# One inversion for four tiles' sums, a bound from sums for w_out on ScalarE, and another order, in attention with two MoE layers

## The chip, the cores and the metric

The kernel runs on one core of one Trainium2 chip. The metric is device time of one execution in microseconds, the median over runs.

## The reference

Queries are averaged in pairs of neighbouring positions, so 1152 positions give 576 queries for each of 4 batches and 8 heads. Attention runs over 1152 keys with head size 64. Its result, 2304 tokens by 512, goes through two layers without a residual.

```
q_pool = q.reshape(B, H, S // 2, 2, D).mean(axis=3)
scores = q_pool @ k.T / sqrt(D);  attn = exp(scores - max(scores))
x = (attn / (sum(attn) + 1e-9)) @ v            # (2304, 512)
h = x @ w_in;   x = (h * sigmoid(h)) @ w_out   # MoE1, 512 -> 2048 -> 512
x = (((x @ w1) * (x @ w2)) @ w3) @ w_out2      # MoE2, 512 -> 1024 -> 1024 -> 512
```

Weights arrive as 64-bit floats. Queries and keys are drawn larger by 5.8 than the rest of the attention's inputs.

## The kernel before

**Numbers.** Most products run on pairs of 16-bit floats, a high and a low part, in three terms: high x high, high x low, low x high. To split a tensor the kernel needs a power of two near its largest magnitude. So a maximum along each partition is taken, TensorE spreads it over the partitions (`top_mm`, L387 and L390), and a scale follows. A weight chunk of 128 x 512 first becomes f32 (`from_f64`): GpSimd L406, ScalarE L412, and two merge instructions on VectorE, L416 and L417. It is then split by ScalarE (L926) and VectorE (L931) and written back by a DMA, 16 chunks for w_in and 16 for w_out (`weights_moe1`). Each chunk's maximum is L903, on VectorE.

**Attention.** A tile is 128 queries of one head, or the 64 last ones of two heads: 144 tiles, 36 for each batch, in groups of four and a fifth in every second group. `tile_ops` gives a tile's steps: scores (TensorE L585, f32, into one of two PSUM tiles `sc` of three banks), the negated maximum over 1152 keys (VectorE L631), the exponential with its running sum (ScalarE L606), one over that sum (VectorE L611 and L614). In the first batch (`whole`) the exponentials stay f32. TensorE transposes them, nine blocks of 128 x 128, into one of the same two `sc` tiles (L643); ScalarE copies the result out (L646); the attention output is a product of 36 f32 matmuls (L677); and the inverses are applied afterwards: four small matmuls spread them over the partitions (L684), ScalarE copies (L697), VectorE multiplies (L702). In the other three batches the inverse scales the split of the exponentials (L652, L617), a DMA transposes them, and the output is L736.

**MoE layers.** A block is 256 tokens, nine blocks in all. `block_ops` makes eight hidden units for each (24 matmuls, L819), the gate by a tanh (ScalarE L835, VectorE L838), the split of the gated values (ScalarE L841, GpSimd L844), and 16 output units (12 matmuls, L860). A hidden unit reads four w_in chunks, an output unit four w_out chunks. MoE2 comes last, in six blocks of 384 tokens: products with w1 and w2 (L1326), w3 times w_out2 computed once (L1183), and the final product (L1404). w1 and w2 are split in two halves of chunks after a spread maximum each; there an Abs with a running sum on ScalarE (L1096) already stands for the maximum.

**What sets the order.** No loop is executed as written. `Plan.op` records every operation with its engine, a cost, a key (its due time, in tiles) and the buffers it reads and writes. `timed` plays the plan through with those costs: on every engine that operation goes next which can start and has the lowest key. `run` does this once with the written keys, and then once for each number of `DRAWS`. A number seeds a random change of the keys: a pull towards the latest time that the last plan allows, an offset for a few kinds of operation, or noise in one stretch. Each pass starts from the keys of the one before it. The order of the last pass is what each engine gets, one queue in program order per engine, DMAs on SyncE's. So a different list gives another order from the first instruction to the last.

```
keys = [o.key for o in self.ops]
order = self.timed(keys)
for n in DRAWS:
    keys = self.draw(n, keys, order)
    order = self.timed(keys)
```

## Time and profile before

| | |
|---|---|
| runs | 1115.26, 1116.67, 1119.01 us (median 1116.67) |
| profiled execution | 1118.18 us; its span, first to last instruction, 1116.4 us |
| TensorE busy | 1071.2 us, 96% |
| VectorE busy | 792.0 us, 71% |
| ScalarE busy | 692.4 us, 62% |
| GpSimd busy | 160.3 us, 14% |
| mean granted clock of TensorE | 0.994 of full speed |

The profile's page shows shares over the whole span. A matmul on the page is one instruction; the weight loads that go with it are PEld and run beside it. The view by stretch cuts the span into windows. The grouped view adds up instructions of one line, operation and shape. The timeline lists an engine's instructions in order of time and joins neighbours of one kind, with their count behind the x. The chain of waits is followed back from the last instruction.

### The profile page before, as it was taken

The numbers are of one execution on the slowest core, as the hardware profiler recorded it, in microseconds if no ns is written. First come the engines' busy times: TensorE is split into PE (matmuls) and PEld (weight loads), VectorE is DVE, ScalarE is ACT, GpSimd is POOL, SyncE is SP. The second block draws the span as 40 slices with busy tenths as digits, with TensorE's granted clock in tenths as the row PEclk, the third lists the DMA queues.
The fourth block names the chain that finished last, engine by engine and source line by source line (L and its number), as shares of the span: only waits on it lengthen the run. The fifth ranks groups of instructions, "written<-read, shape, count | busy, mean of one in ns | idle before, by whom it ended". The sixth has DMA issues, their size and how long they took to land.

```text
span 1116.4 us, 22719 instructions
## 1 busy us (share of the span) xinstructions
PE 1071.2 (96%) x9356; PEld 816.9 (73%) x9356; DVE 792.0 (71%) x1304; ACT 692.4 (62%) x1103; POOL 160.3 (14%) x150
## 2 busy tenths in 40 slices
PE   4877999999999999999999999999999999999998
PEld 4655778888888888788788888788777655555553
DVE  5999997798787897887889784789956442332311
ACT  4767768677776786686687775676656433242322
POOL 1310220021020020020021120546210000000000
PEclk8999999999999999999999999999999999999999
DMA  9855517499998999999989987664530010100001
GB/s 355 263 168 196 190 51 243 91 197 196 199 199 168 188 208 203 207 186 206 202 159 190 168 147 126 218 189 143 189 113 29 29 48 20 38 20 19 19 10 57
DMA packets 294823, 163.21 MB, mean 146 GB/s; under 512 B 256064, under 2 KB 266816, under 8 KB 294720
## 3 DMA queue, kind: packets, MB, share of 16 engines
q1 hardware_dynamic: 294720, 161.77, 60.6%
q8 instruction: 73, 1.20, 0.4%
q14 instruction: 30, 0.25, 0.1%
HBM read 80.22 MB, written 9.44 MB: 80 GB/s over the span
## 4 chain that ended last, share of the span: by engine, by line
PE 53%; DMA 4%; DVE 1%; POOL 1%; issue 0%; ACT 0%; ACTq 0%; POOLq 0%; SPq 0%
PE mt L1326 13%; PE mt L1404 6%; PE mm L819 6%; PE mm L860 6%; PE sc L585 4%; PE mm L1326 4%; PE mm L736 4%; DMA pt<-p 3%; PE mt L1183 3%; PE mt L860 3%; PE mm L1404 2%; PE mt L819 1%; PE mm L1183 1%; DMA v<-in_moe_w_dram 1%; POOL g L844 1%
## 5 line engine op out<-in xcount | busy, mean ns | idle before, releaser
L631 DVE TENSOR_REDUCE sm<-sc 128x1 f32<-128x1152 f32 x144 | 192.2, 1350 | 35.7 <-PE sc L585 35.3
L606 ACT ACTIVATE e<-sc,sm 128x1152 f32<-128x1152 f32 x144 | 175.0, 1216 | 52.7 <-DVE sm L631 43.8
L585 PE MATMUL sc<-kt,qt 64*128 64x384 f32 (+3 forms) x1280 | 183.1, 427 | 17.8 <-ACT pt L646 11.0
L860 PEld LDWEIGHTS <-w 128*128 128x128 f16 x1728 | 166.3, 98 | 31.2 <-issue 11.4
L819 PEld LDWEIGHTS <-w 128*128 128x128 f16 x1728 | 166.4, 98 | 28.2 <-issue 8.6
L844 POOL TENSOR_TENSOR g<-t,g 128x512 f16<-128x512 f32 x72 | 100.4, 1402 | 527.9 <-ACT g L841 475.7
L585 PEld LDWEIGHTS sc<-kt,qt 64*128 64x128 f32 (+1 forms) x1280 | 139.2, 178 | 49.3 <-issue 14.5
L617 DVE SCALAR_TENSOR_TENSOR p<-e,sm,p 128x1152 f16<-128x1152 f32 x108 | 161.2, 1500 | 12.8 <-ACT p L652 12.4
L860 PE MATMUL mm<-g,w 128*128 128x256 f16 x1440 | 167.1, 273 | 0.0
L819 PE MATMUL mm<-x,w 128*128 128x256 f16 x1440 | 165.0, 273 | 1.9 <-DVE x L783 1.0
L652 ACT ACTIVATE p<-e,sm 128x1152 f16<-128x1152 f32 x108 | 134.1, 1251 | 40.6 <-DMA pt<-p 26.0
L736 PE MATMUL mm<-pt,v 128*64 128x256 f16 (+1 forms) x1944 | 89.1, 248 | 3.6 <-DMA pt<-p 3.4
L736 PEld LDWEIGHTS <-v 128*64 128x64 f16 x1944 | 80.7, 111 | 12.3 <-issue 10.8
L1326 PEld LDWEIGHTS <-w1h 128*128 128x128 f16 x576 | 56.1, 98 | 38.3 <-issue 0.8
L1326 PEld LDWEIGHTS <-w2h 128*128 128x128 f16 x576 | 56.0, 98 | 38.2 <-issue 1.4
L1326 PE MATMUL mt<-x2h,w1h 128*128 128x384 f16 x444 | 77.1, 326 | 0.0
L1326 PE MATMUL mt<-x2h,w2h 128*128 128x384 f16 x444 | 76.9, 326 | 0.0
L643 PE MATMUL sc<-identr,e 128*128 128x128 f32 x324 | 44.6, 286 | 14.4 <-ACT e L606 11.3
L835 ACT ACTIVATE t<-mm,xm 128x512 f32<-128x512 f32 x60 | 40.9, 682 | 22.8 <-PE mm L819 20.1
L1345 ACT ACTIVATE asb<-mt,x2m 128x384 f32<-128x384 f32 x37 | 20.8, 577 | 54.4 <-PE mt L1326 48.0
L643 PEld LDWEIGHTS sc<-identr,e 128*128 128x128 f32 x324 | 36.7, 146 | 22.7 <-ACT e L606 14.6
L646 ACT COPY pt<-sc 128x1152 f32<-128x1152 f32 x36 | 40.0, 1116 | 18.8 <-PE sc L643 18.4
(186 smaller groups left out, 1331.4 us busy)
## 6 DMA issues: line engine op xcount, KB each, us to landing
v<-in_moe_w_dram SPq DMA_DIRECT2D x32, 512.0 KB, 4.3
qs<-in_q_dram SPq DMA_DIRECT2D x16, 640.0 KB, 4.8
kt<-in_k_dram SPq DMA_DIRECT2D x16, 576.0 KB, 4.6
qs<-in_q_dram SPq DMA_DIRECT2D x16, 512.0 KB, 4.8
g<-in_moe_w_in_dram SPq DMA_DIRECT2D x16, 512.0 KB, 5.5
w<-t SPq DMA_DIRECT2D x32, 256.0 KB, 2.4
stage<-in_v_dram SPq DMA_DIRECT2D x12, 576.0 KB, 5.1
x2d<-t SPq DMA_DIRECT2D x36, 128.0 KB, 2.4
```

The lines of the kernel that those rows point to most:

```text
L585: return nc.tensor.matmul(sc.t[cols, bank, x0 - bank * (S // 3) : x1 - bank * (S // 3)], qt.t[rows * D : (rows + 1) * D, 4 if last else 2 ...
L606: nc.scalar.activation(e.t.rearrange("p (a x) -> p a x", a=3), flat(), AF.Exp, bias=sm.t[:, 0:1], accum_out=sm.t[:, 1:2])
L617: nc.vector.scalar_tensor_tensor(p16.t[:, 1], e.t, sm.t[:, 3:4], p16.t[:, 0], op0=ALU.mult, op1=ALU.subtract)
L631: DVE, 1.36, lambda: nc.vector.tensor_reduce(sm.t[:, 0:1], flat(), axis=AX.XY, op=ALU.max, negate=True),
L643: nc.tensor.transpose(to[:, c * P : (c + 1) * P], e.t[:, c * P : (c + 1) * P], ident)
L652: ACT, 1.27, lambda: nc.scalar.activation(p16.t[:, 0], e.t, AF.Copy, scale=sm.t[:, 3:4]),
L736: nc.tensor.matmul(ps.t[a * D : (a + 1) * D, :nn], v16.t[:, a, c, tv, :], rhs, start=idx == 0, stop=idx == 3 * NK - 1,)
L819: nc.tensor.matmul(ps.t[:, f % 2 * BL : (f % 2 + 1) * BL], w16[0][ct * NQ + f // 4][:, tw, (f % 4) * P : (f % 4 + 1) * P], x16.t[:, ct, tx ...
L844: nc.gpsimd.tensor_tensor(gv(1), two(g32), gv(0), op=ALU.subtract)
L860: nc.tensor.matmul(ps.t[:, :BL], w16[1][f][:, tw, ct * P : (ct + 1) * P], gs[u].t[:, f % 4, tg, :], start=f == 0 and n == 0, stop=f == NF ...
L1326: nc.tensor.matmul(ps.t[:, :TB], buf.t[:, ct, tw, f * P : (f + 1) * P], xr.t[:, ct, tx, :], start=idx == 0, stop=idx == 11,)
L1404: nc.tensor.matmul(ps.t, ab[f].t[:, ta, m * P : (m + 1) * P], w3_b.t[:, f, tb, :], start=f == 0 and n == 0, stop=f == NF2 - 1 and n == 2,)
```

## The change

Three things change.

The four whole tiles of a group in the first batch write their sums into four columns of one small tile `gs`, and after the fourth, one add and one reciprocal of 128 x 4 stand for four pairs of 128 x 1. The spread reads its columns. The fifth tile of a group, and all tiles of later batches, keep their own pair.

For w_out, the chunk's maximum on VectorE becomes an Abs on ScalarE that sums the row as it goes. The scale is then a power of two from the largest sum over 512 magnitudes, which is at least the largest magnitude. w_in keeps its maximum.

The list of draws is another and longer one, 87 numbers where there were 33.

```diff
--- before.py
+++ after.py
@@ -30,9 +30,15 @@
 LOAD_AFTER = 3.0
 SLACK = 3.0
 DRAWS = (
-    200001, 200004, 200006, 200007, 200012, 200017, 200034, 200040, 200060, 200094, 200118, 200122,
...
+    3000001, 3000002, 3000004, 3000006, 3000008, 3000014, 3000020, 3000032, 3000041, 3000050,
...
 )
 SWITCH = 0.1
 AFTER = {PE: 0.25, ACT: 0.2, DVE: 0.15, POOL: 0.2, SP: 0.0}
@@ -334,7 +340,8 @@
     t_pt = tags(attn, "pt", 3, [P, 2, 2 * NK, P], F16)
     t_x32 = tags(attn, "x32", 1, [P, NP, BL])
     t_x32t = tags(attn, "x32t", 1, [P, NP, BL])
-    t_sm = tags(attn, "sm", 12, [P, 4])
+    t_sm = tags(attn, "sm", 8, [P, 4])
+    t_gs = tags(attn, "gs", 2, [P, 3, 4])
     t_mv = tags(attn, "mv", 2, [P, 6, NP])
     t_rs = tags(attn, "rs", 1, [P, BL])
 
@@ -558,7 +565,7 @@
 
     pts = {}
     x32s = {}
-    dgs = {}
+    dgs, sums = {}, {}
     turns, asked = {}, {}
 
     def pt32(pt):
@@ -602,10 +609,21 @@
                 tc.add_to_no_dep_group(f"bank{paired[0]}", first.ins)
                 tc.declare_fence(second.ins, group=f"bank{paired[0]}")
 
+        joint = whole and not last
+        if joint and (b, g, hp) not in sums:
+            sums[(b, g, hp)] = attn_buf(t_gs)
+        n = 2 * h + j - 2 * g
+
         def soft_exp():
+            to = sums[(b, g, hp)].t[:, 0, n : n + 1] if joint else sm.t[:, 1:2]
             nc.scalar.activation(
-                e.t.rearrange("p (a x) -> p a x", a=3), flat(), AF.Exp, bias=sm.t[:, 0:1], accum_out=sm.t[:, 1:2]
-            )
+                e.t.rearrange("p (a x) -> p a x", a=3), flat(), AF.Exp, bias=sm.t[:, 0:1], accum_out=to
+            )
+
+        def inverses():
+            s_ = sums[(b, g, hp)].t
+            nc.vector.tensor_scalar(s_[:, 1], s_[:, 0], 1e-9, None, op0=ALU.add)
+            nc.vector.reciprocal(s_[:, 2], s_[:, 1])
 
         def inverse():
             nc.vector.tensor_scalar(
@@ -631,11 +649,15 @@
             DVE, 1.36, lambda: nc.vector.tensor_reduce(sm.t[:, 0:1], flat(), axis=AX.XY, op=ALU.max, negate=True),
             [sc], [(sm, 0)], i - 0.5,
         )
-        op(ACT, 1.42, soft_exp, [sc, (sm, 0)], [e, (sm, 1)], i - 3.0 * whole)
-        op(DVE, 0.32, inverse, [(sm, 1)], [(sm, 2)], i + 0.2)
+        op(ACT, 1.42, soft_exp, [sc, (sm, 0)], [e, (sums[(b, g, hp)], n) if joint else (sm, 1)], i - 3.0 * whole)
+        if not joint:
+            op(DVE, 0.32, inverse, [(sm, 1)], [(sm, 2)], i + 0.2)
+        elif n == 3:
+            s_ = sums[(b, g, hp)]
+            op(DVE, 0.32, inverses, [(s_, c) for c in range(4)], [(s_, 9)], i + 0.2)
         if whole:
             st = Buf(t_s)
-            dgs[i] = sm
+            dgs[i] = (sums[(b, g, hp)], n) if joint else (sm, None)
 
             def turn32():
                 to = st.t.rearrange("p a x -> p (a x)")
@@ -679,11 +701,11 @@
                     )
 
         def spread():
-            for (a, jj), dg in inv.items():
+            for (a, jj), (dg, n) in inv.items():
                 cols = slice(a * TAIL, (a + 1) * TAIL) if last else slice(0, P)
                 nc.tensor.matmul(
                     sp.t[a * D : (a + 1) * D, jj * P : jj * P + (TAIL if last else P)],
-                    dg.t[:, 3:4].to_broadcast([P, D]),
+                    (dg.t[:, 3:4] if n is None else dg.t[:, 2, n : n + 1]).to_broadcast([P, D]),
                     ident[:, cols],
                     start=True,
                     stop=True,
@@ -691,7 +713,7 @@
 
         sp, rs = Buf(t_mm), attn_buf(t_rs)
         first = op(
-            PE, 0.3 if last else 0.6, spread, [ident_b] + [(dg, 2) for k_, dg in inv.items() if not last or k_ == (0, 0)],
+            PE, 0.3 if last else 0.6, spread, [ident_b] + [(dg, 2 if n is None else 9) for k_, (dg, n) in inv.items() if k_ == (0, 0)],
             [sp, (rs, 0)], i + 1.0,
         )
         op(ACT, 0.3 if last else 0.45, lambda: nc.scalar.copy(rs.t[:, :nn], sp.t[:, :nn]), [sp], [(rs, 1)], i - SOON)
@@ -898,13 +920,23 @@
 
             op(SP, 0.5, load, [], [(w64, 0), (w64, 1)], key - 3, land=5.5).ready = 45.0 * wi
             from_f64(lambda c=c: whole[c], words, w16_b[wi][c], w64, key)
-            op(
-                DVE, 0.69,
-                lambda c=c: nc.vector.reduce_max(
-                    wmx[wi][:, c : c + 1], whole[c], axis=AX.X, apply_absolute_value=True
-                ),
-                [w16_b[wi][c]], [(wmx_b[wi], c)], key + 0.02,
-            )
+            if wi == 0:
+                op(
+                    DVE, 0.69,
+                    lambda c=c: nc.vector.reduce_max(
+                        wmx[wi][:, c : c + 1], whole[c], axis=AX.X, apply_absolute_value=True
+                    ),
+                    [w16_b[wi][c]], [(wmx_b[wi], c)], key + 0.02,
+                )
+            else:
+                junk = moe_buf(t_t32)
+                op(
+                    ACT, 0.66,
+                    lambda c=c, junk=junk: nc.scalar.activation(
+                        junk.t, whole[c], AF.Abs, accum_out=wmx[wi][:, c : c + 1]
+                    ),
+                    [w16_b[wi][c]], [junk, (wmx_b[wi], c)], key + 0.02,
+                )
             key += step
         s_ = wst[wi]
         op(DVE, 0.2, lambda: nc.vector.reduce_max(s_[:, 0:1], wmx[wi], axis=AX.X), [wmx_b[wi]], [wst_b[wi]], key2)
```

What stands where in the engines' queues changes from the beginning. In the rows below `sc` are the two score tiles, `sm` a tile's small column of maximum, sum and inverse, `e` exponentials, `w_0_n` chunk n of w_in, `g` the 64-bit words of a chunk, `wmx` the column of chunk maxima. First VectorE, around the maxima of the third and fourth tile, before:

```order
L631 TENSOR_REDUCE sm_120<-sc_82 128x1
L416 SCALAR_TENSOR_TENSOR w_0_3_145<-w_0_3_145,g_177 128x512
L417 SCALAR_TENSOR_TENSOR w_0_3_145<-g_177,w_0_3_145 128x512
L416 SCALAR_TENSOR_TENSOR w_0_2_144<-w_0_2_144,g_176 128x512
L417 SCALAR_TENSOR_TENSOR w_0_2_144<-g_176,w_0_2_144 128x512
L611 TENSOR_SCALAR sm_120<-sm_120 128x1
L614 RECIPROCAL sm_120<-sm_120 128x1
L631 TENSOR_REDUCE sm_121<-sc_81 128x1
L631 TENSOR_REDUCE sm_122<-sc_82 128x1
```

and now:

```order
L649 TENSOR_REDUCE sm_120<-sc_81 128x1
L649 TENSOR_REDUCE sm_121<-sc_82 128x1
L423 SCALAR_TENSOR_TENSOR w_0_0_140<-w_0_0_140,g_172 128x512
L424 SCALAR_TENSOR_TENSOR w_0_0_140<-g_172,w_0_0_140 128x512
L926 TENSOR_REDUCE wmx_70<-w_0_0_140 128x1
L625 TENSOR_SCALAR gs_126<-gs_126 128x4
L626 RECIPROCAL gs_126<-gs_126 128x4
L926 TENSOR_REDUCE wmx_70<-w_0_2_142 128x1
L926 TENSOR_REDUCE wmx_70<-w_0_1_141 128x1
```

The pair of one tile's inverse that stood between two maxima is gone; the pair on 128x4 comes once for the four tiles, and maxima now stand in twos.

Next TensorE, from the first transposes on; `identr` is the identity of a transpose or a spread, `kt` and `qt` are keys and queries. Before:

```order
L643 MATMUL sc_81<-identr,e_107 128x128 x9
L585 MATMUL sc_82<-kt_99,qt_97 128x192
L585 MATMUL sc_82<-kt_99,qt_97 128x384 x2
L585 MATMUL sc_82<-kt_99,qt_97 128x192
L643 MATMUL sc_81<-identr,e_108 128x128 x9
L585 MATMUL sc_81<-kt_99,qt_97 128x192
L585 MATMUL sc_81<-kt_99,qt_97 128x384 x2
L585 MATMUL sc_81<-kt_99,qt_97 128x192
L585 MATMUL sc_82<-kt_100,qt_98 128x192
L585 MATMUL sc_82<-kt_100,qt_98 128x384 x2
L585 MATMUL sc_82<-kt_100,qt_98 128x192
```

and now:

```order
L665 MATMUL sc_81<-identr,e_107 128x128 x9
L665 MATMUL sc_82<-identr,e_108 128x128 x9
L592 MATMUL sc_81<-kt_99,qt_97 128x192
L592 MATMUL sc_81<-kt_99,qt_97 128x384 x2
L592 MATMUL sc_81<-kt_99,qt_97 128x192
L592 MATMUL sc_82<-kt_99,qt_97 128x192
L592 MATMUL sc_82<-kt_99,qt_97 128x384 x2
L592 MATMUL sc_82<-kt_99,qt_97 128x192
L665 MATMUL sc_81<-identr,e_109 128x128 x9
L665 MATMUL sc_82<-identr,e_107 128x128 x9
L706 MATMUL mm_83<-identr,gs_126 64x128 x4
```

Score tiles and transposes alternated one by one, and now go by twos; the spread is one row of four matmuls on `gs`.

Last VectorE where MoE2's second weights get their scale; `ws_1` is that scale, `x2m` a block's scale, `wfb` and `v` a chunk of other weights, `w3t` a split row of w3, `w2h` the split w2. Before:

```order
L390 TENSOR_REDUCE ws_1_190<-mm_84 128x1
L376 TENSOR_SCALAR ws_1_190<-ws_1_190 128x1
L377 TENSOR_SCALAR ws_1_190<-ws_1_190 128x1
L380 TENSOR_SCALAR ws_1_190<-ws_1_190 128x1
L1057 TENSOR_SCALAR ws_1_190<-ws_1_190 128x1
L1058 TENSOR_SCALAR ws_1_190<-ws_1_190 128x1
L1298 TENSOR_SCALAR x2m_7980<-x2m_7980,ws_1_190 128x1
L1290 TENSOR_REDUCE x2m_7981<-x2s 128x1
L1168 TENSOR_TENSOR w3t_9058<-wfb_7977,w3t_9058 128x4x128
L1071 SCALAR_TENSOR_TENSOR w2h<-w_2_7960,ws_1_190,w2h 128x512
```

and now:

```order
L397 TENSOR_REDUCE ws_1_188<-mt_7922 128x1
L423 SCALAR_TENSOR_TENSOR wfb_7952<-wfb_7952,v_2_7947 128x512
L424 SCALAR_TENSOR_TENSOR wfb_7952<-v_2_7947,wfb_7952 128x512
L383 TENSOR_SCALAR ws_1_188<-ws_1_188 128x1
L384 TENSOR_SCALAR ws_1_188<-ws_1_188 128x1
L387 TENSOR_SCALAR ws_1_188<-ws_1_188 128x1
L1089 TENSOR_SCALAR ws_1_188<-ws_1_188 128x1
L1090 TENSOR_SCALAR ws_1_188<-ws_1_188 128x1
L1330 TENSOR_SCALAR x2m_7955<-x2m_7955,ws_1_188 128x1
L423 SCALAR_TENSOR_TENSOR wfb_7950<-wfb_7950,v_0_7945 128x512
L424 SCALAR_TENSOR_TENSOR wfb_7950<-v_0_7945,wfb_7950 128x512
L1103 SCALAR_TENSOR_TENSOR w2h<-w_1_7934,ws_1_188,w2h 128x512
```

Between the scale and the first split there was a reduction over a block and a split of w3; now two merges of other weights stand there.

## Rows read from the trace of the kernel before

**Rows 1.** page: busy us of each engine, share, instructions

```profile
PE 1071.2 (96%) x9356; PEld 816.9 (73%) x9356; DVE 792.0 (71%) x1304; ACT 692.4 (62%) x1103; POOL 160.3 (14%) x150
```

**Rows 2.** by stretch: length, busy us of each engine, clock, DMA share, GB/s

```profile
14.00:112.00 98.00, 77.63 (x586) 58.87 (x586) 93.24 (x164) 71.05 (x104) 17.20 (x22) 0.95 0.68 234
112.00:168.00 56.00, 53.32 (x506) 42.82 (x504) 51.92 (x102) 40.65 (x61) 14.37 (x14) 1.00 0.35 120
...
190.00:300.00 110.00, 109.18 (x1080) 91.71 (x1079) 90.60 (x147) 78.41 (x107) 12.24 (x8) 1.00 0.86 170
300.00:700.00 400.00, 395.92 (x4448) 336.43 (x4447) 329.43 (x498) 287.46 (x402) 55.77 (x40) 1.00 0.94 182
```

**Rows 3.** VectorE groups, 0-191 us: xcount | busy us, mean ns | idle before

```profile
L631 DVE TENSOR_REDUCE sm<-sc 128x1 f32<-128x1152 f32 x36 | 48.3, 1350 | 6.3 <-PE sc L585 6.1
...
L903 DVE TENSOR_REDUCE wmx<-w 128x1 f32<-128x512 f32 x32 | 20.6, 675 | 0.1
...
L614 DVE RECIPROCAL sm<-sm 128x1 f32<-128x1 f32 x35 | 5.7, 164 | 1.2
...
L611 DVE TENSOR_SCALAR sm<-sm 128x1 f32<-128x1 f32 x35 | 5.1, 144 | 1.3 <-ACT e L606 1.2
```

**Rows 4.** TensorE's waits: us in total, times, longest us

```profile
PE sc L643 <- ACT e L606: 11.3, 8, 4.0
...
PE mm L736 <- DMA pt<-p: 3.4, 4, 1.3
```

**Rows 5.** VectorE timeline, maxima of tiles 20 and 32: start us, us

```profile
97.62 1.35 DVE L631 TENSOR_REDUCE sm<-sc 128x1 f32<-128x1152 f32 x1
...
167.74 1.35 DVE L631 TENSOR_REDUCE sm<-sc 128x1 f32<-128x1152 f32 x1
```

**Rows 6.** TensorE timeline: an attention output, transposes of tiles 20 and 31

```profile
34.34 4.11 PE L677 MATMUL mm<-pt,v 128*64 128x256 f32 x36
...
103.64 1.20 PE L643 MATMUL sc<-identr,e 128*128 128x128 f32 x9 [1.47 <-ACT pt L646]
...
173.25 2.18 PE L643 MATMUL sc<-identr,e 128*128 128x128 f32 x18
```

**Rows 7.** groups on VectorE, whole span, one on four columns

```profile
L536 DVE TENSOR_SCALAR mv<-mv,xm 128x4 f32<-128x4 f32 x3 | 0.7, 222 | 0.0
```

**Rows 8.** groups on ScalarE, whole span: an Abs with a running sum

```profile
L1096 ACT ACTIVATE wfb<-w 128x512 f32<-128x512 f32 x16 | 10.0, 628 | 10.0 <-DVE w L417 9.9
...
L1096 ACT ACTIVATION_READ_ACCUMULATOR wfb<-w 128x1 f32 x16 | 3.0, 188 | 0.0
```

**Rows 9.** page, DMA issues: write-back of a split chunk, KB, us

```profile
w<-t SPq DMA_DIRECT2D x32, 256.0 KB, 2.4
```

**Rows 10.** chain that ended last, 480 to 520 us: start us, us, what

```profile
481.56 2.14 PE sc L585 x12
...
489.50 1.17 PE sc L585 x6
...
499.90 4.04 PE mm L860 x36
...
505.10 1.42 PE mm L860 x12
```

**Rows 11.** VectorE timeline: w2 spread maximum read, second to fourth split

```profile
785.56 0.28 DVE L390 TENSOR_REDUCE ws<-mm 128x1 f32<-128x128 f32 x1
...
794.36 2.08 DVE L1071 SCALAR_TENSOR_TENSOR w2h<-w,ws,w2h 128x512 f16<-128x512 f32 x3
```

**Rows 12.** TensorE timeline: spread for w2, products with w1, with w2

```profile
784.20 0.39 PE L387 MATMUL mm<-identr,ws 128*128 128x128 f32 x2
...
788.32 4.06 PE L1326 MATMUL mt<-x2h,w1h 128*128 128x384 f16 x24
...
797.74 2.45 PE L1326 MATMUL mt<-x2h,w2h 128*128 128x384 f16 x14
```

**Rows 13.** page, costliest groups: the score maxima over the whole span

```profile
L631 DVE TENSOR_REDUCE sm<-sc 128x1 f32<-128x1152 f32 x144 | 192.2, 1350 | 35.7 <-PE sc L585 35.3
```

10 rows, old and new, of the table DRAWS are left out of this document.

## The prediction

> **What bounds the kernel now.** I read the page's busy shares first. TensorE is busy for 96% of the span and VectorE for 71% [rows 1], so in the mean TensorE leads. Then the table by stretch, because that mean covers two regimes [rows 2]. From 14 to 112 us VectorE is busy 93.24 of 98 us and TensorE 77.63; from 112 to 168 it is 51.92 against 53.32 of 56. After 190 us TensorE is full (109.18 of 110, 395.92 of 400) and VectorE is not. So the first 168 us belong to VectorE, the rest to TensorE: what VectorE saves counts only early, and what TensorE saves counts later.
>
> VectorE's early work is 36 maxima over a score tile (48.3 us), 32 maxima over weight chunks (20.6), and small inverses [rows 3]. TensorE's own waits agree: the longest, 11.3 us, are transposes that wait for an exponential [rows 4], a link of the chain score, maximum, exponential, transpose, copy.
>
> To turn this into a price I count two things up to the same point: VectorE's instructions in its program order, each at its mean duration from the grouped view, and TensorE's work in its own order at the unit prices below. "Lost" is a point's time less TensorE's work before it. Up to the maximum of tile 20 VectorE has 145 instructions, 95.2 us by their means; it ends at 97.62 + 1.35 = 98.97. Up to that of tile 32 it has 271, 168.5 us, and ends at 167.74 + 1.35 = 169.09 [rows 5]. So clock time is the sum plus 3.8 us, later plus 0.6: the start of 9 us, less the small overlap of neighbours. VectorE has had no rest worth counting. TensorE's unit prices are 0.97 us a score tile and 0.20 a run of them (below), 1.13 for nine transposes (18 took 2.18), 4.0 for 36 matmuls of the first batch's attention output (36 took 4.11), 0.49 a spread, 1.31 for 12 plain matmuls. The transposes of tile 20 start at 103.64 after 64.9 us of work (21 score tiles 24.3, 19 transposes 21.5, 4 outputs 16.0, spreads and small ones 3.1), those of tile 31 at 173.25 after 130.6 [rows 6]. Lost is 38.7 us at the first point and 42.6 at the second, so the VectorE regime costs some 42.6 us in all.
>
> **The change, part by part.** *Inverses.* 32 tiles of the first batch lose an add (144 ns) and a reciprocal (164 ns) each [rows 3]: 32 x 0.308 = 9.9 us off VectorE. Eight pairs on 128x4 come back. The trace has no such reciprocal. The nearest row is a 128x4 TENSOR_SCALAR, 222 ns, with a scalar from memory [rows 7]. Bounds are 8 x 0.308 = 2.5 us and 8 x 2 x 0.222 = 3.6; I take 2.6, near the lower, since four columns are little beside what a single one costs. Net 7.3 us. The spread (L684) now waits for one pair after the fourth sum. Queued behind it on TensorE are the scores of the next pair. The order puts that spread after the transposes of tiles three and four, which themselves need the exponentials that write those sums, so I cost the wait at nothing; uncovered, it is the pair's 0.33 us eight times, those 2.6 us again.
>
> *The maxima of w_out.* 16 x 0.675 = 10.8 us leave VectorE [rows 3]. ScalarE gets 16 Abs with a running sum. The same form stands in the trace for the next layer: 628 ns, and 188 ns to read the accumulator [rows 8], so 16 x 0.816 = 13.1 us; the lower bound is the 628 alone, 10.0 us. The cover is ScalarE's idle time, 154 - 71.05 - 40.65 = 42.3 us between 14 and 168 us [rows 2]. The scratch tile is one of five shared buffers, written once and let go, so it holds nothing up by itself.
>
> A rule speaks against this part. On chip, the maximum costs 675 ns and the Abs 816. The Trainium skill (ScalarE: Activation LUTs, Rules for kernel authors) sends max and its like to VectorE, up to about three times faster per element in bf16. By the rule the move is a loss, here 16 x 0.14 = 2.3 us if one path held both; by the rows the two engines are not equally loaded, and the place decides. The trace agrees with the direction and not with a factor of three, the data being f32.
>
> *The order in the first batch.* TensorE's program now takes tiles in pairs, two scores and two transposes. I repeat the count. Up to the maximum of tile 24 VectorE has 159 instructions, 117.6 us; with the offset between those of rows 5 (3.4) that ends at 121.0. Those are 24 maxima (32.4 us), 54 merges (43.7), 16 maxima of w_in (10.8), 15 splits (11.4), 12 inverses (1.9) and 38 others (17.3). TensorE has 85.5 us of work before those transposes: 24 score tiles in 14 runs (26.6), 23 sets of transposes (26.0), 6 attention outputs (21.2), 6 spreads (2.7), 3 hidden units (8.1), 4 small ones (0.9). The difference is 35.5; before, tile 20 had 98.97 - 64.9 = 34.1 and tile 32, with 131.7 us of work, 37.4. From that maximum to the transposes' start took 4.7 us at tile 20 (103.64 - 98.97). I add it: lost is 40.2 us at tile 24. From there the new order only gains slack: at tile 32 VectorE has 149.9 us where it had 168.5, TensorE 128.6 us where it had 131.7, so the difference is 152.1 - 128.6 = 23.5. The later growth of lost, 38.7 to 42.6, should go. Gain 42.6 - 40.2 = 2.4 us. It is far below the 18.1 us taken off VectorE, because the new order puts more VectorE work (54 merge instructions against 48, 15 splits against 4) ahead of its tightest tile. Bounds: 0, if the pairs wait as the singles did, to 4.
>
> What is late next is the last quarter of w_out's split. Its last chunk ends at about 173.5 us on VectorE; a write-back of 2.4 us follows [rows 9], and TensorE has 142.7 us of work before the unit that reads it: 33.2 lost, inside the 40.2.
>
> *The order of kinds of matmul.* In the trace one score tile alone takes 1.17 us and two in a row 2.14, so the second takes 0.97; 12 output matmuls take 1.42 and 36 take 4.04, so each 12 after the first take 1.31 [rows 10]. A run of scores costs 0.20 us once, a run of plain matmuls 0.11, and I price a run of attention outputs like the latter. Counted in the two orders, runs of scores go from 110 to 91, of plain ones from 90 to 79, of attention outputs from 35 to 32: 19 x 0.20 + 11 x 0.11 + 3 x 0.11 = 5.3 us that TensorE does not work. Lost time is counted against that work, so the gains add. Lower bound 2.4, the runs after the first batch alone (7, 6 and 3).
>
> *The second weights of MoE2.* Here a wait tightens. Before, the matmul that spreads w2's maximum ran at 784.20 and the first product with w2 at 797.74, while VectorE's fourth half ended at 794.36 + 2.08 = 796.44 [rows 11, 12]: 1.3 us to spare. Four products with w1 and a unit of 24 matmuls stood between. Now four w1 products come ahead of the spread, and two with that unit stand between. Two fewer, at 4.06 us the pair [rows 12], leave 13.5 - 4.1 = 9.4 us. VectorE took 796.44 - 785.56 = 10.9 us from its read to the fourth half; its new list there adds up to some 7.9. So this costs between 0 and 10.9 + 1.4 - 9.4 = 2.9 us. I take 1.5. Queued behind are the remaining products and, through them, everything to the end.
>
> **Sum.** The profiled execution took 1118.18 us, with a span of 1116.4. Off come 2.4 and 5.3, on go 1.5: -6.2, so 1112.0 for that execution. The median of the runs is 1.5 below the profiled one, so 1110.5.
>
> **Rivals.** *The waits grow elsewhere.* In the stage from 190 us on TensorE loses little, 0.8 + 4.1 us up to 700 [rows 2]. A wholly new order may double that: 1110.5 + 4.9 = 1115.4, which is no change that can be told. For it: waits on a transposing DMA are there now (3.4 us in four) [rows 4], and all of them move. Against: between a group's last scores and its attention output the new order has 15.3 us of TensorE work at the least, the old 15.0, and more in the middle.
>
> *ScalarE takes over (slower).* Its place is the stretch from tile 10 to 32, where all 16 Abs now stand. If its 42.3 us of idle time are waits that do not shrink, the transposes of tile 31 come 13.1 us after 173.25, at 186.3, with 127.4 us of work before them. Lost 58.9 instead of 42.6, so +16.3 - 5.3 = +11.0 and 1127.7. It decides from lost 42.6 + 5.3 = 47.9, transposes at 175.3: TensorE would be ready at 127.4 + 40.2 = 167.6, so once ScalarE is 7.7 us late. For it: by tile 32 ScalarE's work sums to 139 us in the new order, 127 in the old, hardly less than VectorE's 150. Against: most of its idle time is waiting for VectorE and TensorE, which come earlier.
>
> *VectorE binds to the end.* Then all 18.1 us come off: 1098.6. Against it VectorE idles 35.3 us before score maxima waiting for TensorE, 6.1 of that before 191 us [rows 3, 13]. For it stands the weight-load share of 73% [rows 1]. The Trainium skill (Perfetto Trace Analysis, Identifying the Most-Contended Engine) calls matmul busy time a poor measure and prefers that share; by it TensorE would have a quarter to spare. The trace does not bear that out after 190 us, where 0.7 to 1% of a stretch is left idle.
>
> **How the numbers follow.** Forecast 0.62, with its own range 1105 to 1114; growing waits 0.20; ScalarE 0.12; VectorE to the end 0.05; 0.01 for none. A difference below 0.3% (3.35 us, so 1113.3 to 1120.0) can't be told from no change. Faster: 0.59 of the forecast, the 0.05, and 0.05 of the growing waits, 0.69. Same: 0.03 + 0.15 + 0.01 = 0.19. Slower: 0.12. The range leaves out ScalarE's case and the far end of the last: 1104 to 1118.5.
>
> **What would show it.** Right: VectorE's sum by stretch falls by about 18 us before 190 us; TensorE is full from about 125 us on instead of 168; score runs cost 0.20 each and there are 91. Wrong: ScalarE busy over 90% between 60 and 160 us with exponentials waiting behind an Abs; first w2 product idle over 3 us behind VectorE; waits on transposing DMAs well above 3.4 us; or TensorE's busy sum not lower by some 5 us.

## The result, and the profile after

The changed kernel takes 1104.11 us (median of 5 runs, 1102.12 to 1105.36) where the kernel before took 1116.67 in the same comparison: a ratio of 0.9886, with a 95% interval of 0.9868 to 0.9903, so 12.6 us less. The forecast was 6.2 us less. The sign is as forecast; the size is twice what was worked out. The time lies below the forecast's own range of 1105 to 1114 us and 0.1 us inside the wider one of 1104 to 1118.5. That it falls inside is luck, as the sum missed by 6.4 us. The profiled execution took 1105.23 us, its span 1103.4, 13.0 less than before.

The page, busy us of each engine, answers [rows 1]:

```profile
PE 1066.8 (97%) x9356; PEld 820.9 (74%) x9356; DVE 779.3 (71%) x1240; ACT 704.5 (64%) x1135; POOL 161.9 (15%) x150
```

By stretch, with the columns of [rows 2], of the kernel after:

```profile
14.00:112.00 98.00, 79.97 (x595) 62.40 (x594) 91.59 (x135) 76.35 (x119) 18.26 (x23) 0.91 0.66 233
112.00:168.00 56.00, 55.37 (x546) 46.20 (x546) 45.37 (x80) 49.82 (x85) 14.79 (x13) 1.00 0.44 152
168.00:190.00 22.00, 19.27 (x192) 16.54 (x193) 16.61 (x29) 17.34 (x25) 0.00 (x0) 1.00 0.68 236
190.00:300.00 110.00, 109.82 (x1065) 92.34 (x1064) 90.27 (x145) 76.03 (x105) 10.50 (x9) 1.00 0.85 162
300.00:700.00 400.00, 396.95 (x4480) 340.00 (x4478) 330.81 (x498) 291.60 (x407) 60.56 (x45) 1.00 0.96 188
700.00:800.00 100.00, 100.00 (x815) 83.78 (x813) 92.64 (x129) 68.45 (x134) 50.22 (x46) 1.00 0.56 185
```

TensorE is nearly full from 112 to 168 us (55.37 of 56, against 53.32), but not from there to 190 (19.27 of 22; before, 21.96): around there it waits 2.3 us for ScalarE's copies of transposes and 0.9 us for a write-back of w_out. The last row has no partner in [rows 2], because the table there ended at 700 us. These are the kernel before's rows for it: the same stretch, and three pieces of it.

```profile
700.00:800.00 100.00, 97.57 (x823) 83.19 (x821) 86.69 (x121) 70.18 (x135) 49.60 (x47) 0.98 0.59 192
...
712.00:720.80 8.80, 8.80 (x82) 7.80 (x80) 8.73 (x10) 6.73 (x15) 5.99 (x6) 1.00 0.46 144
720.80:723.40 2.60, 0.17 (x2) 0.09 (x1) 2.57 (x3) 1.62 (x4) 2.44 (x3) 0.96 0.36 132
723.40:726.60 3.20, 3.20 (x16) 2.21 (x16) 3.13 (x5) 1.89 (x5) 1.30 (x2) 0.50 0.65 204
```

Before, TensorE stood still for 2.43 us at 720.9 us, and from 723.2 to 726.6 its granted clock was 0.50, the 1.2 GHz level: 16 matmuls in 3.2 us where the stretch before has 82 in 8.8. After has neither. The timeline of TensorE before shows what the stall waited for, a low part of the hidden units from GpSimd:

```profile
717.98 2.78 PE L819 MATMUL mt<-x,w 128*128 128x256 f16 x24
720.60 0.27 PE L860 MATMUL mt<-g,w 128*128 128x256 f16 x1
723.31 2.50 PE L860 MATMUL mt<-g,w 128*128 128x256 f16 x11 [2.43 <-POOL g L844]
```

The list of TensorE's waits, of which [rows 4] shows two lines, held it too:

```profile
PE mt L860 <- POOL g L844: 2.4, 1, 2.4
```

TensorE's waits after, as in [rows 4]:

```profile
PE sc L665 <- ACT e L619: 14.3, 10, 4.5
PE sc L592 <- ACT pt L668: 7.0, 9, 2.5
PE sc L592 <- DVE qt L475: 6.7, 1, 6.7
PE mm L758 <- DMA pt<-p: 2.4, 4, 1.6
PE mm L882 <- DMA w<-t: 0.9, 1, 0.9
```

Lost time (a point's time less TensorE's work before it, as in the prediction) at four points, and the work, all from the two timelines:

```
                                    before   after    difference
lost at MoE1's 10th output unit      41.8     40.3      -1.5   (194.5 and 195.0 us)
grown up to its 110th                 8.5      7.5      -1.0   (to 687.5 and 679.3 us)
grown up to its 125th                 4.5      0.2      -4.3   (to 739.4 and 730.2 us)
grown up to TensorE's last matmul     0.3      0.4      +0.1
TensorE's work                     1056.8   1051.4      -5.4
last matmul ends                   1111.9   1099.8     -12.1
```

The span fell by 13.0 us; the 0.9 us that the table leaves lie behind the last matmul.

How far a single trace can be trusted here: two kernels below that are the changed one up to 188 us show 38.2 and 41.2 us at that tenth unit. This scatter goes with the granted clock of the first batch. From 14 to 112 us its mean was 0.97 in the trace with 38.2, and 0.91 in the one with 41.2 and in after's (40.3): TensorE stood at 0.50 there for some 7 us in the first and some 17 us in the other two. Two kernels below that are the kernel before up to 700 us show the same. They start the transposes of tile 20 at 101.96 us (clock 0.97) and 104.43 us (0.93), where before starts them at 103.64 (0.95). So differences of lost time under some 3 us in the first batch are not told apart by one profile, and the -1.5 can't be told from nothing. The stall and the work are. The clock does not favour the changed kernel: its five runs had mean granted clocks of 0.992 to 0.998, runs of the kernel before 0.991 to 0.998.

### The profile page after: what moved, and what is told of

It is laid out like the page before. It is cut to its first block, busy times and chain, and to the rows that moved or that the text cites. A ratio compares the mean times of both kernels' runs of the same rounds, so it can differ in the third digit from the quotient of the medians.

```text
span 1103.4 us, 22722 instructions
## 1 busy us (share of the span) xinstructions
PE 1066.8 (97%) x9356; PEld 820.9 (74%) x9356; DVE 779.3 (71%) x1240; ACT 704.5 (64%) x1135; POOL 161.9 (15%) x150
## 4 chain that ended last, share of the span: by engine, by line
PE 80%; DMA 9%; DVE 6%; ACT 3%; issue 2%; SPq 0%; ACTq 0%; DVEq 0%
PE mm L841 13%; PE mt L1358 12%; PE sc L592 11%; PE mm L882 10%; DMA pt<-p 7%; PE mm L758 6%; PE mt L1436 6%; PE mm L1358 5%; PE mt L882 3%; PE mt L1215 2%; PE mt L841 2%; PE mm L1436 2%; PE mm L699 2%; DVE sm L649 2%; PE sc L665 2%
## 5 line engine op out<-in xcount | busy, mean ns | idle before, releaser
L619 ACT ACTIVATE e<-sc,sm 128x1152 f32<-128x1152 f32 x144 | 175.2, 1217 | 53.0 <-DVE sm L649 41.2
L592 PE MATMUL sc<-kt,qt 64*128 64x384 f32 (+3 forms) x1280 | 180.8, 427 | 14.3 <-ACT pt L668 7.0
L841 PE MATMUL mm<-x,w 128*128 128x256 f16 x1488 | 170.0, 273 | 0.0
L1358 PEld LDWEIGHTS <-w2h 128*128 128x128 f16 x576 | 56.1, 98 | 37.6 <-issue 0.8
L1358 PE MATMUL mt<-x2h,w2h 128*128 128x384 f16 x420 | 72.5, 326 | 0.0
L1358 PE MATMUL mt<-x2h,w1h 128*128 128x384 f16 x420 | 72.4, 326 | 0.0
L665 PE MATMUL sc<-identr,e 128*128 128x128 f32 x324 | 44.9, 294 | 14.4 <-ACT e L619 14.3
L665 PEld LDWEIGHTS sc<-identr,e 128*128 128x128 f32 x324 | 39.3, 152 | 19.9 <-ACT e L619 18.2
L860 DVE SCALAR_TENSOR_TENSOR t<-t,mm 128x512 f32<-128x512 f32 x62 | 42.3, 683 | 14.0 <-ACT t L857 13.8
```

Of the source, the lines that this page charges most:

```text
L592: return nc.tensor.matmul(sc.t[cols, bank, x0 - bank * (S // 3) : x1 - bank * (S // 3)], qt.t[rows * D : (rows + 1) * D, 4 if last else 2 ...
L619: nc.scalar.activation(e.t.rearrange("p (a x) -> p a x", a=3), flat(), AF.Exp, bias=sm.t[:, 0:1], accum_out=to)
L665: nc.tensor.transpose(to[:, c * P : (c + 1) * P], e.t[:, c * P : (c + 1) * P], ident)
L841: nc.tensor.matmul(ps.t[:, f % 2 * BL : (f % 2 + 1) * BL], w16[0][ct * NQ + f // 4][:, tw, (f % 4) * P : (f % 4 + 1) * P], x16.t[:, ct, tx ...
L1358: nc.tensor.matmul(ps.t[:, :TB], buf.t[:, ct, tw, f * P : (f + 1) * P], xr.t[:, ct, tx, :], start=idx == 0, stop=idx == 11,)
```

## The experiments

All but four keep one kernel's order of all instructions and change only what is named. Each was timed against the kernel before on its chip, so kernels are compared by their ratios to it; a thousandth is 1.1 us.

**The two parts without the new order, and the new order without the parts.** In the kernel before:

```
+ accum_out=gs[:, 0, n_ : n_ + 1]              # one tile of sums for each group of four
+ if len(done[(b, g, hp)]) == 4: one add, one reciprocal on 128x4
+ wi == 1: nc.scalar.activation(..., AF.Abs, accum_out=wmx[wi][:, c : c + 1])   # at the maximum's place
```

> The kernel before with its own order of all instructions, and only the two parts put in: each group of four tiles of the first batch keeps its sums in one tile and gets one add and one reciprocal after the fourth sum; the 16 maxima of w_out stand at their old places as Abs with a running sum on ScalarE. TensorE's order of kinds is the old one, so nothing comes from fewer runs. Theory (VectorE's list up to the tightest tile sets what the first batch costs, the rest of the gain is the order): VectorE's sum up to the maximum of tile 20 falls by 4.4 us, up to that of tile 32 by 18, so the tightest tile moves from 31 to 20 and lost time goes from 42.6 to about 34.4: 8 us faster than before, about 1108.5, and 4 us slower than the changed kernel; the stall of 2.4 us and the half clock near 720 us stay. Rival 1 (the order alone made the gain): within 2 us of before. Rival 2 (all that leaves VectorE is gained): 18 us faster than before, faster than the changed kernel.

Measured: ratio 1.0014 (0.9999 to 1.0030), no gain. In the trace lost was 34.9 us at tile 20 (34.4 expected), where three traces with the kernel before's first batch have 37.0 to 39.5. It stood at 35.0 at tile 26; by the transposes of tile 31 it was 41.0, where those three have 40.8 to 42.9. The stretch from 136 to 158 us, columns as in [rows 2], of this kernel:

```profile
136.00:158.00 22.00, 18.99 (x190) 14.89 (x190) 8.06 (x12) 21.44 (x49) 5.48 (x6) 1.00 0.07 26
```

and of the kernel before:

```profile
136.00:158.00 22.00, 20.93 (x183) 16.91 (x182) 20.23 (x37) 14.88 (x23) 5.99 (x6) 1.00 0.24 76
```

ScalarE is now busy 21.44 of 22 us and VectorE 8.06: the old order has these maxima side by side, so on ScalarE they become a block. An extract of its timeline shows an exponential between them; TensorE's transposes that need the one at 152.54 waited 1.69 us.

```profile
148.77 0.63 ACT L918 ACTIVATE p<-w 128x512 f32<-128x512 f32 x1
149.31 0.19 ACT L918 ACTIVATION_READ_ACCUMULATOR p<-w 128x1 f32 x1
149.40 1.20 ACT L610 ACTIVATE e<-sc,sm 128x1152 f32<-128x1152 f32 x1
150.50 0.19 ACT L610 ACTIVATION_READ_ACCUMULATOR e<-sc,sm 128x1 f32 x1
150.60 0.62 ACT L918 ACTIVATE p<-w 128x512 f32<-128x512 f32 x1
...
152.54 1.21 ACT L610 ACTIVATE e<-sc,sm 128x1152 f32<-128x1152 f32 x1
```

So what the first tiles gain is gone by then, and the theory's time fails: it had not counted ScalarE there. This is the prediction's rival "ScalarE takes over" in the old order; the next two sections of runs bear on it.

In the changed kernel, its order kept, parts were taken back: single pairs emitted where each sum comes ready, and the maximum in the lambda of the sum.

```
+ nc.vector.tensor_scalar(s_[:, 1, c : c + 1], s_[:, 0, c : c + 1], 1e-9, None, op0=ALU.add)
+ nc.vector.reciprocal(s_[:, 2, c : c + 1], s_[:, 1, c : c + 1])
- nc.scalar.activation(junk.t, whole[c], AF.Abs, accum_out=wmx[wi][:, c : c + 1])
+ nc.vector.reduce_max(wmx[wi][:, c : c + 1], whole[c], axis=AX.X, apply_absolute_value=True)
```

> The changed kernel's order of all instructions, with both parts taken back: 32 single adds and reciprocals at the places where their sums come ready, and the 16 maxima of w_out as maxima on VectorE where the sums stood on ScalarE. TensorE's order is that of the changed kernel, so the fewer runs stay. Theory: VectorE's sum rises by 4.8 us up to tile 24 and by about 16 up to tile 30 (32.3 + 9.4 = 41.7 us ahead of TensorE's work, then 0.6 and 4.7), lost is about 46.5 where the same count gave 40.2: 6.5 us slower than the changed kernel (5 to 9), so still 6 faster than before. Rival 1 (the order alone): within 1.5 us of the changed kernel. Rival 2 (all of VectorE's saving is gained): 18 us slower than the changed kernel, slower than before.

> The changed kernel's order, with only the single adds and reciprocals back (32 pairs where there were 8), the w_out sums staying on ScalarE. Theory: 4.8 us more on VectorE up to tile 24, its tightest: about 4.8 us slower than the changed kernel (2 to 5). Rival 1 (the order alone): within 1 us. Rival 2: 7.3 us slower.

> The changed kernel's order, with only the 16 maxima of w_out back on VectorE at the same places, the joint inverses staying. Theory: nothing is added before tile 24, about 9.4 us up to tile 30, where the sum then stands 35.9 us ahead of TensorE's work and 0.6 and 4.7 come on top: lost 41.2 against 40.2, so 1 us slower than the changed kernel (0 to 4); this part of the change is worth little by itself. Rival 1 (the order alone): within 1 us. Rival 2: 10.8 us slower. Rival 3 (ScalarE is what binds after tile 24, and the move cost time): faster than the changed kernel by 1 to 3 us.

Measured: 0.9946 (0.9930 to 0.9962) with both back, 0.9914 (0.9898 to 0.9930) with the inverses back, 0.9939 (0.9924 to 0.9953) with the maxima back. Against the changed kernel's 0.9886 that is +6.7, +3.1 and +5.9 us, each uncertain by some 2.7, as it is a difference between two chips' comparisons. The first two are near the theory (6.5 and 4.8). The third is not (1): the text took it that no sum of w_out stands before tile 24 in the new order, but the first runs at 52.3 us and eleven of the 16 before that tile's maximum ends at 121.1. TensorE's waits up to 190 us, of the kernel with the maxima back:

```profile
PE sc L665 <- ACT e L619: 20.1, 9, 5.1
PE sc L592 <- DVE qt L475: 6.8, 1, 6.8
PE sc L592 <- ACT pt L668: 5.5, 11, 1.7
```

The transposes wait 20.1 us for exponentials where after has 14.3, and lost at tile 24 is 41.2 instead of 37.9 us; with both back 41.9. With the inverses back it is 37.6, no more than in after, though at a granted clock of 0.97 from 14 to 112 us against 0.91: that trace does not show the inverses' 3.1 us. One stretch is steadier than the sums from the start: from the transposes of tile 19 to those of tile 24 it takes 27.4 to 27.8 us in after, in the two traces that share its first batch and with the inverses back, but 29.7 with the maxima back and 30.2 with both. So the maxima do cost time ahead of tile 24, the place that the prediction named. From there to the tenth output unit 2.0 to 3.2 us more are lost in each of the four. By time the new order alone is worth some 6 us, the parts some 7 in it and nothing in the old one; the profiled execution with both back is only 2.4 us longer than after's, being the shortest of its six (1107.66 us, median 1109.7).

**Why nothing in the old one.** The same edit in the kernel before, once with the inverses alone and once with every second sum on ScalarE (`wi == 0 or c % 2` keeps the maximum).

> The kernel before with its own order, and only the joint inverses put in (8 adds and reciprocals for 32); the maxima of w_out stay on VectorE. It is to say why both parts together gave nothing in the old order. Theory: up to tile 20 the inverses gave 3.8 us of lost time (38.7 to 34.9 in the two traces), and by tile 32 the 16 Abs, which the old order packs into 21 us in which ScalarE does not rest, took it back (35.0 at tile 26, 41.0 at tile 32). Without the Abs on ScalarE the inverses' saving stays, lost is about 36 at tile 32 as VectorE's sum there falls by 7 (42.6 before): 4 to 6 us faster than before. Rival 1 (in the old order whatever leaves VectorE early is given back later, whoever does the maxima): within 2 us of before.

> The kernel before with its own order, the joint inverses, and every second of the 16 maxima of w_out as a sum on ScalarE, the other 8 staying maxima on VectorE. Theory (all 16 made ScalarE run without a rest for 20 us between tiles 26 and 32 and cost what the inverses gave): with 8 ScalarE has some 6.5 us less in that stretch, lost stays at 36 to 37 up to tile 32, 4.5 to 6 us faster than before. Rival 1 (each Abs on ScalarE costs its share, evenly): half way between the inverses alone and both parts, 1 to 2.5 us faster than before. Rival 2: the same as before.

Measured: 0.9958 (0.9945 to 0.9970), 4.7 us faster, for the inverses alone; 0.9972 (0.9956 to 0.9989), 3.1 us faster, with half of the sums. By time the first bears the theory out: in the old order the 16 sums cost the 4.7 us that the inverses give, and a little more. Its trace shows only a part: lost is 39.7 us at tile 31 where some 36 was expected, before 42.6. By time the second lies between the theory (4.5 to 6) and its first rival (1 to 2.5), and its interval reaches both; from 136 to 158 us ScalarE is busy 18.55 us there, and lost at tile 31 is 41.9, not 36 to 37.

The stretch in which the sums stand tells more. From the transposes of tile 26 to those of tile 31 the three traces with the kernel before's first batch agree within 0.01 us:

```
                          us from tile 26 to 31   TensorE idle in it   ScalarE busy
before, and two like it          28.5                    2.2              19.8
inverses alone                   28.3                    2.1              19.8
and half of the sums             28.8                    2.4              23.4
and all 16 sums                  31.5                    4.8              28.6
```

All 16 sums cost 3.3 us there, every second one 0.5. So they do not cost evenly: the block costs where it fills ScalarE (28.6 of 31.5 us). The rest of the 6 us by time is not located.

**The stall at 720 us.** In the kernel before, queue positions alone:

```
+ ACT:  the high part (g_hi) of the unit that was waited for, three places earlier
+ POOL: its low part (g_lo), three places earlier
```

> The kernel before, with two instructions moved by three and four places in their queues: the high part of one block's half of the hidden units on ScalarE and its low part on GpSimd, the one that MoE1's output unit waits 2.43 us for at 720.9 us; it now stands ahead of two splittings of weight bytes and of another low part that is read later. Nothing else moves. Theory: the stall goes, and with it the stretch at 1.2 GHz that follows at 734 us: 2.4 to 4.1 us faster than before. Rival 1: TensorE waits as long a few units later for the low part that was put behind: within 1 us of before. Rival 2: the stall goes and the half clock does not: 2.4 us.

Measured: 0.9980 (0.9969 to 0.9991), 2.2 us. (The half clock begins at 723.2 us, not at 734 as the text has it.) From 700 to 800 us one wait was left, a new one, and the granted clock stayed at 1.00:

```profile
PE mt L893 <- POOL g L877: 1.4, 1, 1.4
```

Then the tanh, the gate and the high part of the next unit went forward too:

> The kernel before, as in the run with the two instructions moved, and three more moved ahead near 720 us: the sigmoid part, the gate and the high part of the next hidden unit, each ahead of one splitting or merge of MoE2's weights. It takes away the 1.40 us that TensorE still waited at 727.4 us in that run. Theory (the stretch cost 2.43 us of stall and 1.7 us of half clock, both lost to the end): 4.1 us faster than before, no stall over 1 us between 700 and 800 us and no half clock there. Rival (only the stall counts, or the time comes back as other waits): no more than the 2.2 us of the first run.

Measured: 0.9971 (0.9955 to 0.9988), 3.2 us, the interval 1.3 to 5.0. TensorE's row for the stretch has no wait left:

```profile
700.00:800.00 100.00, 100.00 (x832) 85.38 (x831) 92.70 (x127) 71.44 (x140) 51.40 (x48) 1.00 0.59 192
```

Lost grew 0.2 us from the 110th to the 125th unit, as after, where before had 4.5. So that row of the table in the section on the result is this stall and its half clock. By time the interval holds the 4.1 and also the 2.2, so that the half clock's 1.7 us come back in full is read from the trace only.

**The price of a run.** The changed kernel with TensorE's order changed after 188 us, other queues kept: at 30 places `Q Q U` became `Q U Q` (Q a score tile, U a unit of MoE1 or an attention output).

> The changed kernel, with TensorE's order changed at 30 places after 188 us: where two score tiles stand together and a unit of MoE1 or an attention output follows, the second score tile comes after it. The other queues keep their orders. Theory (a run of scores costs 0.20 us, one of plain matmuls or outputs 0.11): 30 runs of scores more, 19 of plain ones, 2 of outputs: 30 x 0.20 + 21 x 0.11 = 8.3 us slower than the changed kernel, if no wait grows. Rival 1 (the order of kinds costs nothing, and the 5.3 us of the forecast's second term came from elsewhere): within 1.5 us of it. Rival 2 (scores that come 1.3 to 2.9 us later make VectorE late): over 12 us slower, with waits for exponentials or transposing DMAs in the trace.

Measured: 0.9990 (0.9977 to 1.0004), 11.6 us slower than the changed kernel. TensorE's groups from 186 us to 800 (line, shapes, xcount | busy us, mean ns | idle before):

```profile
L915 PE MATMUL mm<-g,w 128*128 128x256 f16 x1369 | 160.4, 273 | 1.1 <-DMA w<-t 1.0
L874 PE MATMUL mm<-x,w 128*128 128x256 f16 x1296 | 148.8, 273 | 0.8 <-DVE t L893 0.4 <-ACT x32t L817 0.4
L625 PE MATMUL sc<-kt,qt 64*128 64x192 f32 (+1 forms) x960 | 139.2, 425 | 0.1
L791 PE MATMUL mm<-pt,v 128*64 128x256 f16 (+1 forms) x1944 | 89.9, 248 | 5.4 <-DMA pt<-p 2.9 <-DVE t L893 2.1 <-ACT t L927 0.4
```

The same groups of the changed kernel, from 188 us:

```profile
L882 PE MATMUL mm<-g,w 128*128 128x256 f16 x1371 | 158.2, 273 | 0.9 <-DMA w<-t 0.9
L841 PE MATMUL mm<-x,w 128*128 128x256 f16 x1296 | 148.0, 273 | 0.0
L592 PE MATMUL sc<-kt,qt 64*128 64x192 f32 (+1 forms) x960 | 132.7, 420 | 0.7 <-ACT e L619 0.7
L758 PE MATMUL mm<-pt,v 128*64 128x256 f16 (+1 forms) x1944 | 88.5, 248 | 2.6 <-DMA pt<-p 2.4
```

The scores take 6.5 us more, 0.22 for each of 30 runs. (A group's busy time overlaps its neighbours' at each change of kind, so the four groups' 10.9 us are more than the engine's.) From the tenth output unit to the last matmul this kernel takes 11.2 us more (192.9 to 1108.9 against 195.0 to 1099.8); its waits from 190 to 800 us sum to 6.2 against 3.1, which leaves 8.1 of work, and 8.3 was priced. The 11.6 us by time are that and the waits, which the price had left out. The mean of one score matmul hardly moves (420 to 425 ns): the price of a run is read from a group's sum. The other way round, at 9 places a single score tile went behind the unit after it, to the next one:

> The changed kernel, with TensorE's order changed at 9 places after 188 us the other way: a single score tile that one or two units stand in front of another single one goes behind them, so that the two run together. Theory: 9 runs of scores, 3 of plain matmuls and 1 of outputs less: 9 x 0.20 + 4 x 0.11 = 2.2 us faster than the changed kernel, so faster than both. Rival 1 (order of kinds costs nothing): the same. Rival 2 (the delayed tile's chain gets late): slower.

Measured: 0.9951 (0.9937 to 0.9965), 7.3 us slower than the changed kernel, though its scores are busy about a microsecond less. TensorE's timeline and its granted clock by stretch show one of the places:

```profile
637.43 2.21 PE L625 MATMUL sc<-kt,qt 64*128 64x192 f32 x16
642.86 4.45 PE L874 MATMUL mm<-x,w 128*128 128x256 f16 x24 [3.22 <-DVE t L893]
```

```profile
639.00:643.00 4.00, 0.78 (x7) 0.54 (x6) 3.56 (x7) 2.80 (x4) 0.00 (x0) 1.00 0.09 18
643.00:647.00 4.00, 4.00 (x23) 2.96 (x22) 3.74 (x4) 2.99 (x5) 1.40 (x2) 0.57 0.99 185
```

A hidden unit waited 3.22 us for a gate on VectorE, and half clock followed. VectorE itself had waited 5.14 us for the paired scores: their maximum started at 638.74 us, the exponential on ScalarE, which had waited 4.73 us for it, at 640.20, the unit's tanh, queued behind that, at 641.41, and the gate at 642.12. From 190 to 800 us TensorE's waits sum to 10.2 us against the changed kernel's 3.1. That is rival 2 of this run.

**More of the same.** The changed kernel with the maxima of w_in on ScalarE as well, all 16 or every second.

> The changed kernel's order, with the 16 maxima of w_in too as sums of absolute values on ScalarE, at the same places: 10.8 us more off VectorE, all before tile 17, and 13.1 us more on ScalarE. Theory: up to the exponential of tile 24 ScalarE's instructions in the trace after sum to 103.9 us and that ends at 122.4, so 18.5 us of rest, some 8 of it the start; 13.1 us more fill it, while VectorE's 117.6 us come down to 106.8. The two are then equal, and nothing is gained: within 3 us of the changed kernel. Rival 1 (VectorE alone sets the first batch): 8 to 10 us faster than the changed kernel. Rival 2 (ScalarE binds at once, as in the old order with all sums): over 3 us slower.

> The changed kernel's order, with every second maximum of w_in as a sum on ScalarE: 5.4 us less on VectorE, 6.5 more on ScalarE. Theory: VectorE still leads up to tile 24 (112.2 us against ScalarE's 110.4), lost falls by 2 to 4 us: 1 to 4 us faster than the changed kernel. Rival 1 (waits along the chain score, maximum, exponential set it, not either engine's sum): no change within 1.5 us. Rival 2: slower, as the exponentials wait behind the sums.

Measured: 0.9881 (0.9861 to 0.9900) and 0.9874 (0.9853 to 0.9894), both the changed kernel's time within what can be told. From 14 to 112 us, with all 16, columns as before:

```profile
14.00:112.00 98.00, 79.21 (x648) 60.65 (x647) 84.77 (x129) 88.73 (x157) 17.46 (x23) 0.98 0.69 241
```

VectorE is down to 84.77 and ScalarE up to 88.73 us: the two have changed places. Lost at tile 24 was 34.9 against 37.9 us, but that is no gain: the kernel with 30 places changed, which is the changed one up to there, has 35.4, and both were granted more clock than after (0.98 and 0.97 from 14 to 112 us). Later, from the 30th to the 57th output unit, 3.0 us more were lost (152.8 us against 149.9). The half measure's forecast of 1 to 4 us and its rival of none can't be told apart. Neither of the two is shown to beat the changed kernel.

## Why the prediction was right in sign and wrong in size

- *VectorE's saving.* Right in kind: the eight pairs take 163 and 178 ns for an add and a reciprocal, 2.7 us where 2.6 was taken; the sums 630 and 189 ns, as forecast. VectorE's durations sum to 16.3 us less over the span, not 18.1, other instructions having become 1.5 longer; its busy time, overlaps counted once, is 12.7 less. The sign that the prediction named, some 18 us less before 190 us, did not come: busy time there fell by 10.9 (169.7 to 158.8). In the new order the parts are worth some 7 us by time, in the old none.
- *The order in the first batch (-2.4).* The count of VectorE held: its maximum of tile 24 was to end at 121.0 us and ends at 119.79 + 1.35 = 121.14. Lost was to be 40.2 at tile 24 and was 37.9, as the transposes started 2.3 us behind that maximum where 4.7 had been taken over from tile 20:

```profile
119.79 1.35 DVE L649 TENSOR_REDUCE sm<-sc 128x1 f32<-128x1152 f32 x1
...
123.41 1.15 PE L665 MATMUL sc<-identr,e 128*128 128x128 f32 x9
```

"From there the new order only gains slack" failed: lost rose to 40.3 by the tenth output unit, by the waits around 168 to 190 us, one of them for the w_out write-back that the prediction had covered. So -1.5 at 195 us, too near the scatter to set against 2.4. Behind it may be two larger numbers of opposite sign: the order without the parts loses 43.9 us there, 2.1 more than before, and the parts take that and more off again; but 2.1 is inside the scatter too.
- *Runs of kinds (-5.3).* Right: 0.22 us a run of scores by the experiment, where 0.20 was read, and 8.1 us for the whole edit, where 8.3 was priced. The work in the two orders differs by 5.4 us at these prices. TensorE's busy sum fell by 4.4 (1071.2 to 1066.8); that sum contains time at 0.50, and half of this is 6.2 us before and 8.0 after. Without it the fall is 6.2.
- *MoE2's second weights (+1.5).* It didn't happen. TensorE's timeline after has, without a wait:

```profile
779.97 0.38 PE L394 MATMUL mt<-identr,ws 128*128 128x128 f32 x2
...
789.62 2.11 PE L1358 MATMUL mt<-x2h,w2h 128*128 128x384 f16 x12
```

VectorE read the maximum at 780.39 and ended the fourth half at 787.70:

```profile
780.39 0.29 DVE L397 TENSOR_REDUCE ws<-mt 128x1 f32<-128x128 f32 x1 [1.32 <-PE mt L394]
...
784.57 3.13 DVE L1103 SCALAR_TENSOR_TENSOR w2h<-w,ws,w2h 128x512 f16<-128x512 f32 x4
```

The distance is 9.65 us (9.4 forecast), VectorE's list 7.3 (7.9 counted): 1.9 us to spare. The middle between that list and the old duration of 10.9 was the wrong choice, since a count of what stands there was at hand.

- *What failed.* The step "in the stage from 190 us on TensorE loses little, 0.8 + 4.1 us up to 700", which let the later stage enter only as a rival on the slow side. The table ended 20 us before the largest wait after the first batch: 2.43 us of stall and 3.4 us at half clock at 720.9 us, 4.3 us of lost time, all in the trace of before. The three kernels above that keep the old order there and leave it alone have the stall too (2.31 to 2.83 us), two of them with half clock behind it. The new order lost it. Taken away in the old order, it gave 3.2 us by time (1.3 to 5.0). With this term at -4.3, the +1.5 at 0 and the first batch at -1.5, the sum is -1.5 - 5.4 - 4.3 = -11.2; the stage up to 700 us gave 1.0 more, where the rival had feared a loss of 4.9.
- *Rivals.* The waits did not grow (transposing DMAs 2.4 us in four, before 3.4). ScalarE didn't take over in the new order (busy 85.3 of 100 us from 60 to 160 us, where over 90% was named as a sign), but does in the old one. VectorE doesn't bind to the end: from 190 to 800 us TensorE waits 3.1 us in all. The Trainium skill's rule (ScalarE: Activation LUTs, Rules for kernel authors) that max goes to VectorE was weighed against the part: by the runs it is right in the old order, where all 16 on ScalarE cost 1.0014 - 0.9958 = 0.56%, 6.3 us, and wrong in the new, where they gain 5.9, each uncertain by some 2 to 3. In these two cases the engine that rests at that place decides, not the price of the instruction.

## What to carry to other kernels

When a change gives a kernel a new order, list every wait of the engine that bounds it over the whole span, as each can go as well as come, and add to each long one the half clock that follows it, if one does. Price a moved instruction at the stretch where it lands: side by side on the receiving engine, 16 sums cost 6 us, spread over 100 us they gained 6. A chain ordered by hand or by a planner is worth measuring before it is "improved": pairing nine score tiles saved about 1 us of score time and lost 7. And where the start scatters from execution to execution, compare traces between two fixed points behind it: a stretch of the first batch took 28.5 us in three traces, within 0.01, while the time at which it began differed by 2.1.

## What was not expected of the hardware

TensorE's granted clock fell to 0.50 for 3.4 us (once 6.8) at the end of stalls, or right after them, in otherwise full stretches: after 2.43 us in the kernel before, 2.31 with both parts in the old order, 2.83 with the inverses alone, 3.22 in the paired one. After 2.38 us in the kernel with half of the sums it did not, and with all sums of w_in on ScalarE it fell at 388.2 us, at the end of stalls of only 1.30 and 0.78 us. So it goes with stalls, and their length alone does not say when.

In the first batch, where TensorE waits often, the same instructions were run at 0.50 for some 7 us in one execution and some 17 in another, and the tenth output unit came 3.0 us later in the second (192.9 and 195.9 us).
